# Softplus by one ScalarE function instead of six operations, and the sign of the weights by one VectorE operation, in a retention layer followed by two feed-forward layers

## The chip, the cores and the metric

One core of a Trainium2 chip runs the whole program. The metric is the device time of one launch in microseconds (us), lower is better. The core's engines work side by side, each on its own list of instructions in a fixed order: TensorE (PE) multiplies matrices into PSUM banks, with its weight loads on a row of their own (PEld), VectorE (DVE) and ScalarE (ACT) do the elementwise work, SyncE (SP) issues the DMAs, and GpSimd (POOL) does next to nothing here. An instruction at the head of an engine's list that waits for a semaphore holds up everything behind it on that engine.

## The reference, cut to what matters

```python
# q, k, v: [4, 8, 576, 64]; weights [512, 2048] and [2048, 512], drawn as 64-bit floats
scores = q @ k.transpose(0, 1, 3, 2) / sqrt(64)
ret = (scores * D[None]) @ v               # D[h, i, j] = gamma_h ** (i - j) for i >= j, else 0
x = ret.transpose(0, 2, 1, 3).reshape(2304, 512)
h = x @ moe_w_in
x = (maximum(h, 0) + log1p(exp(-abs(h)))) @ moe_w_out      # softplus
r = maximum(x @ moe2_w_in, 0)
out = (r * r) @ moe2_w_out
```

## The kernel before, in words

The retention runs in chunks of 64 tokens with a carried state. In the first layer every fp32 operand is split into a high part that TensorE's fp32r format holds and a low rest, and a product is three matmuls (high by high, low by high, high by low). Tokens go in five tiles of 512 or 384 (`TILES`). For a tile the work is 16 steps, one for each block of 128 hidden units: `g1` makes a block of h in a PSUM bank named `ph` (12 matmuls), softplus turns it into g, `split_g` into `gh` and `gl`, and `g2` adds it to four output sums named `acc` (12 matmuls). `step` writes this order down by hand: `g1` of step j, softplus of j, a visit to the retention, `split_g` of j - 1, `g2` of j - 2, then weights. The first tile is done in two halves, with the second tile between them, so the order of the tiles is 0 (blocks 0 to 7), 1, 0 (blocks 8 to 15), 2, 3, 4. All but tile 4 is in a manual schedule, where each engine keeps the written order; for tile 4 and what follows, a scheduler picks it.

A visit (`visit`) does one chunk of the retention among the steps: small matmuls `pb` (scores, L388), `po` (outputs, L436) and `st` (state, L413), on VectorE the mask `ring<-pb` (L398), the product `xr<-po` (L459) and the scaling of v (L369, in place in `ring`), and on ScalarE the copy of the state (L424). `pb` takes the PSUM bank that the next `ph` will have, so a bank goes from a block of h to scores and back.

Weights come as 64-bit floats. `words` turns a staged pair of 32-bit words into fp32: ScalarE scales the high word, and multiplies it by a further -2^32 where it is negative (parametric ReLU, L152); ScalarE makes the low bits (L153); VectorE shifts and joins them (L157). `split_w` then makes the high part on ScalarE (L185) and the low part on VectorE (L186). Weights of the second layer go the same way (`split_s`, `split_o`) during tiles 0 to 4. A staging tile (`wi_raw`, `wo_raw`, three buffers) is free for its next load after L157. SP issues these loads and those of `ring` in one queue. In the steps of the first half tile two blocks of weights are made per step, later one or less.

Softplus before is three ScalarE functions in `softplus_a` (Abs L525, Exp L526, Ln L527) and three VectorE operations in `softplus_b` (L532, L535, L538, of which L538 reads `ph` again). Ln writes to tile `l`, a pair of buffers that `drain_one` also uses for stores to DRAM (`xo`).

The last part (`second_phase`) is the second layer, seven products instead of eight by a Strassen scheme. Its code isn't touched.

Of the kernel before, what the change touches and what calls it, by code (L numbers as in the profile page):

```python
# [7 lines left out]
F32 = mybir.dt.float32  # L8
# [3 lines left out]
AF = mybir.ActivationFunctionType  # L12
ALU = mybir.AluOpType
# [3 lines left out]
P = 128  # L17
# [28 lines left out]
def kernel(  # L46
# [26 lines left out]
    nc = tc.nc  # L73
# [19 lines left out]
    ew = ctx.enter_context(tc.tile_pool(name="ew", bufs=2))  # L93
# [14 lines left out]
    below_one = cst[:, C_ONE:C_ONE + 1]  # L108
# [31 lines left out]
    def words(t, ct):  # L140

        y, up, low = t.bitcast(F32)[:, :, 1], t[:, :, 1], t[:, :, 0]
        halves = t.bitcast(U16).rearrange("p a (b two) -> p a b two", two=2)  # L150
        half = halves[:, :, 0, 1]
        nc.scalar.activation(out=y, in_=y, func=AF.Prelu, scale=2.0**-112, alpha=-(2.0**32))  # L152
        nc.scalar.activation(  # L153
            out=low, in_=half, func=AF.Identity, bias=round_up, scale=7.0 / 65535
        )
        yield
        nc.vector.scalar_tensor_tensor(  # L157
            out=ct, in0=up, scalar=3, in1=low,
            op0=ALU.logical_shift_left, op1=ALU.bitwise_or,
        )  # L160
        yield
# [149 lines left out]
    def pump_end():  # L311
        for made in begun:
            while not next(made):
                pass
            pump_load(n_used[0] + STAGES)
        begun.clear()
# [167 lines left out]
    hps = {}  # L484
    tmp = {}
# [27 lines left out]
                ph[:, :n], lhsT=a, rhs=x, start=(j == 0), stop=(j == len(todo) - 1)  # L513
            )

    def softplus_a(key, n):

        ph = hps[key]
        e = ew.tile([P, 512], F32, tag="e", name="e", bufs=3)[:, :n]
        l = ew.tile([P, 512], F32, tag="l", name="l")[:, :n]
        nc.scalar.activation(out=e, in_=ph[:, :n], func=AF.Abs)  # L525
        nc.scalar.activation(out=e, in_=e, func=AF.Exp, scale=-1.0)  # L526
        nc.scalar.activation(out=l, in_=e, func=AF.Ln, bias=below_one, scale=1.0 + 2.0**-23)  # L527
        tmp[key] = (l, e)

    def softplus_b(key, n):  # L530
        l, e = tmp.pop(key)
        nc.vector.scalar_tensor_tensor(  # L532
            out=e, in0=e, scalar=-2.0, in1=e, op0=ALU.add, op1=ALU.mult
        )
        nc.vector.scalar_tensor_tensor(  # L535
            out=l, in0=e, scalar=-0.5, in1=l, op0=ALU.mult, op1=ALU.max
        )
        nc.vector.scalar_tensor_tensor(  # L538
            out=e, in0=hps.pop(key)[:, :n], scalar=0.0, in1=l, op0=ALU.max, op1=ALU.add
        )  # L540
        tmp[key] = e

    def split_g(key, n):
        g = tmp.pop(key)
# [605 lines left out]
    with tc.manual_schedule():  # L1150
# [8 lines left out]
        early_kv(1)  # L1159
        for r in (0, CN):  # L1160
            nc.scalar.dma_start(out=rows_in[r:r + 1], in_=consts[r:r + 1, C_XW:])
        nc.scalar.preload_act_table_set("natural_log_exp_and_others")
        for c in range(2, last):
            early_qk(c)
            early_kv(c)
# [131 lines left out]
    def attend(at_s, i):  # L1297
        rest = None
        while tick[0] < visits(at_s, i):
            if rest:  # L1300
                rest()
            rest = visit(*divmod(tick[0], 2))
            tick[0] += 1
        return rest
# [13 lines left out]
    def step(j, at_s, i):  # L1318
        b, f0, f1 = segments[at_s]
        f = f0 + i  # L1320
        t0, n = TILES[b]
        ends = f == f1 - 1
        if j == 0:
            early_g1(1)
        else:
            g1(j, f, n)
        if at_s == 0 and i < FH - 1:
            pump_end()
        low = []
        if ends and b < last_b:  # L1330
            b1 = segments[at_s + 1][0]
            low = split_x(x_raw.pop(b1), TILES[b1][1])
        softplus_a(j, n)
        later = attend(at_s, i)
        if False and j:
            split_g(j - 1, TILES[steps[j - 1][0]][1])
        for fn in low:
            fn()
        softplus_b(j, n)
        if j and not (False):  # L1340
            split_g(j - 1, TILES[steps[j - 1][0]][1])
        if later:
            later()
        done = g2_parts(j - 2) if j >= 2 else None
        pump_end()
        pump_to(j)
        if j == 0:
            load_chunk(last + 1)
        if done:
            done()  # L1350
        if at_s == 1 and f == KF - 3:
            reload_x()
        if at_s >= 2 and i not in (1, 2):
            n_steps[0] += 1
            goal = -(-18 * NP * n_steps[0] // 46)
            while n_taken[0] < min(18 * NP, goal):
                pump_step()
                n_taken[0] += 1
        if at_s == 3 and i == 0:
            for o in range(KD):  # L1360
                reload_part(o)
        if b == last_b:
            if f == 0:
                second_buffers()
                load_raw(0)
                load_s(4)
            if ends:
                assert n_split[0] == len(items) and not splitting
            for m in range(7):
                if f == GROUP * (m // 2) + GROUP + 1 + m % 2:  # L1370
                    build_t(m)
# [14 lines left out]
    j = len(steps)  # L1386
# [79 lines left out]
```

## Time and profile before

| | |
|---|---|
| three runs | 841.48, 840.74, 837.81 us (median 840.74) |
| profiled execution, first to last instruction (span) | 839.0 us; no time around it is given |
| PE busy | 818.2 us (98%) |
| DVE busy | 702.2 us (84%) |
| ACT busy | 475.3 us (57%) |
| 16 DMA engines, the main queue's share | 71.3% |
| chain of work that ended last | PE 78%, DVE 8%, ACT 8%, DMA 3%, issue 2% |

Busy times are sums over the program, which has stages with different limits; a matmul's end is modelled and overlaps the next one's start, so 98% isn't PE at its peak. PEclk is the granted share of TensorE's clock (0.50 is 1.2 GHz, 1.00 is 2.4 GHz). In a timeline, square brackets hold the time for which the engine was idle before an instruction, and what ended it. Where an instruction waits for several things, the profile names the one that came last by its records.

### The profile page before, as it was taken

To read this page: it belongs to the slowest core of one execution; us is meant where nothing else is said; L and a number is where in the kernel's file an instruction comes from. 1 tells how busy PE (TensorE), PEld (TensorE's weight loads), DVE (VectorE), ACT (ScalarE), POOL (GpSimd) and SP (SyncE) were. 2 spreads that over 40 slices of the span, in tenths; PEclk is the share of its full clock that TensorE was granted. 3 is DMA by queue.
4 is the path that set the end of the run, shared out by engine and by line. 5 is a ranking of instruction groups with operands and counts; after the bars stand their busy time and mean duration, and the time that the engine had idled before them with its cause. 6 is when DMAs were issued, how large, how long until landed. Compare 5 with 4: busy or idle time off the path is not lost.

```text
span 839.0 us, 16498 instructions
## 1 busy us (share of the span) xinstructions
PE 818.2 (98%) x5957; PEld 722.6 (86%) x5957; DVE 702.2 (84%) x1336; ACT 475.3 (57%) x899; POOL 0.2 (0%) x4
## 2 busy tenths in 40 slices
PE   8899999999999998999999999999999999999998
PEld 5677799888788876888799999988999988999887
DVE  4889887878988887787999988999698997787886
ACT  3889888757567667676888521355321554111453
POOL 0000000000000000000000000000000000000000
PEclk9999999999999999999999999999999999999999
DMA  9866544546656665466676688898988889988885
GB/s 234 298 195 235 167 141 145 176 152 214 210 174 198 224 190 176 149 227 202 210 255 219 221 253 249 259 296 275 301 257 245 255 263 280 284 254 252 254 268 176
DMA packets 122804, 189.39 MB, mean 226 GB/s; under 512 B 10466, under 2 KB 68450, under 8 KB 122722
## 3 DMA queue, kind: packets, MB, share of 16 engines
q1 hardware_dynamic: 122560, 188.26, 71.3%
q8 instruction: 47, 0.77, 0.4%
q14 instruction: 33, 0.27, 0.1%
q10 hardware_dynamic: 164, 0.09, 0.1%
HBM read 147.41 MB, written 40.89 MB: 224 GB/s over the span
## 4 chain that ended last, share of the span: by engine, by line
PE 78%; DVE 8%; ACT 8%; DMA 3%; issue 2%; SPq 0%; DVEq 0%; ACTq 0%
PE acc L563 17%; PE ph L512 16%; PE py L699 9%; PE py L772 9%; PE px L699 6%; PE pz L772 6%; PE px L772 6%; PE pz L699 6%; ACT l L527 1%; DMA wi_raw<-in_moe_w_in_dram 1%; DVE l L535 1%; DVE e L532 1%; ACT e L526 1%; ACT e L525 1%; PE po L436 1%
## 5 line engine op out<-in xcount | busy, mean ns | idle before, releaser
L512 PE MATMUL ph<-xh,wi 128*128 128x512 f32 (+1 forms) x632 | 145.1, 371 | 2.2 <-ACT l L527 1.1
L512 PEld LDWEIGHTS ph<-xh,wi 128*128 128x128 f32 x632 | 116.3, 189 | 18.7 <-issue 1.4
L563 PE MATMUL acc<-gl,woh 128*128 128x512 f32 (+1 forms) x320 | 119.0, 372 | 2.9 <-DVE gl L548 2.9
L563 PE MATMUL acc<-gh,woh 128*128 128x512 f32 (+1 forms) x320 | 120.5, 380 | 0.5 <-ACT woh L185 0.5
L563 PE MATMUL acc<-gh,wol 128*128 128x512 f32 (+1 forms) x320 | 118.7, 371 | 0.7 <-DVE wol L186 0.7
L532 DVE SCALAR_TENSOR_TENSOR e<-e 128x512 f32<-128x512 f32 (+1 forms) x80 | 51.0, 638 | 48.7 <-ACT l L527 47.8
L699 PE MATMUL py<-t,sring 128*128 128x384 f32 x432 | 88.6, 339 | 0.0
L525 ACT ACTIVATE e<-ph 128x512 f32<-128x512 f32 (+1 forms) x80 | 44.2, 553 | 60.9 <-PE ph L512 60.4
L512 PE MATMUL ph<-xl,wi 128*128 128x512 f32 (+1 forms) x316 | 77.9, 367 | 0.1
L699 PEld LDWEIGHTS py<-t,sring 128*128 128x128 f32 x432 | 74.8, 188 | 2.6 <-DVE uring L903 0.7
L563 PEld LDWEIGHTS acc<-gl,woh 128*128 128x128 f32 x320 | 60.4, 189 | 12.1 <-DVE gl L548 5.1
L752 ACT CAST gh<-g 128x384 fp32r<-128x384 f32 x84 | 43.1, 515 | 46.6 <-PE px L772 16.7
L563 PEld LDWEIGHTS acc<-gh,woh 128*128 128x128 f32 x320 | 60.4, 189 | 9.8 <-ACT woh L185 0.8
L563 PEld LDWEIGHTS acc<-gh,wol 128*128 128x128 f32 x320 | 60.5, 189 | 8.7 <-DVE wol L186 1.0
L752 ACT CAST gring<-g 128x384 fp32r<-128x384 f32 x84 | 43.1, 514 | 40.3 <-PE py L772 16.4
L512 PEld LDWEIGHTS ph<-xl,wi 128*128 128x128 f32 x316 | 58.1, 188 | 8.0 <-DVE xl L479 0.4
L899 ACT COPY uring<-px 128x384 f32<-128x384 f32 x24 | 11.5, 481 | 87.5 <-PE px L699 87.5
L699 PE MATMUL pz<-t,sring 128*128 128x384 f32 x288 | 58.4, 334 | 0.0
L699 PE MATMUL px<-t,sring 128*128 128x384 f32 x288 | 58.0, 335 | 0.0
L527 ACT ACTIVATE l<-e,cst 128x512 f32<-128x512 f32 (+1 forms) x80 | 54.4, 681 | 5.8 <-DMA x2d<-xo 3.6
L720 DVE TENSOR_TENSOR gring<-g,gring 128x384 fp32r<-128x384 f32 x84 | 46.2, 553 | 10.0 <-ACT gring L752 8.9
L720 DVE TENSOR_TENSOR gl<-g,gh 128x384 fp32r<-128x384 f32 x84 | 46.4, 554 | 9.2 <-ACT gh L752 8.0
(126 smaller groups left out, 1622.3 us busy)
## 6 DMA issues: line engine op xcount, KB each, us to landing
sring<-s2d SPq DMA_DIRECT2D x168, 256.0 KB, 3.2
sring<-o2d SPq DMA_DIRECT2D x168, 256.0 KB, 3.4
wi_raw<-in_moe_w_in_dram SPq DMA_DIRECT2D x32, 512.0 KB, 5.0
wo_raw<-in_moe_w_out_dram SPq DMA_DIRECT2D x32, 512.0 KB, 4.1
s2d<-ct SPq DMA_DIRECT2D x48, 256.0 KB, 2.7
o2d<-ct SPq DMA_DIRECT2D x48, 256.0 KB, 2.6
ring<-in_qk_t_dram SPq DMA_DIRECT2D x14, 512.0 KB, 4.8
ring<-in_kv_dram SPq DMA_DIRECT2D x14, 512.0 KB, 6.1
```

The source lines that it names most:

```text
L436: nc.tensor.matmul(po[(LO, HI)[hh % 2], hh // 2, :], lhsT=before[rows, hh, :] if carried else sv[:, hh, :], rhs=qp[:, hh, :] if carried el ...
L512: nc.tensor.matmul(ph[:, :n], lhsT=a, rhs=x, start=(j == 0), stop=(j == len(todo) - 1))
L525: nc.scalar.activation(out=e, in_=ph[:, :n], func=AF.Abs)
L526: nc.scalar.activation(out=e, in_=e, func=AF.Exp, scale=-1.0)
L527: nc.scalar.activation(out=l, in_=e, func=AF.Ln, bias=below_one, scale=1.0 + 2.0**-23)
L532: nc.vector.scalar_tensor_tensor(out=e, in0=e, scalar=-2.0, in1=e, op0=ALU.add, op1=ALU.mult)
L563: nc.tensor.matmul(acc[j][:, :n], lhsT=a, rhs=x, start=(begin and m == 0), stop=(end and m == 2))
L699: nc.tensor.matmul(ps, lhsT=a, rhs=x, start=(first and m == 0), stop=(m == len(todo) - 1), skip_group_check=True,)
L720: nc.vector.tensor_tensor(out=out, in0=a, in1=b, op=ALU.subtract)
L752: nc.scalar.copy(h, src)
L772: nc.tensor.matmul(blocks[m][:, :cols], lhsT=a[:, c], rhs=x, start=(first and p == n == 0), stop=(p == NP - 1 and n == len(todo) - 1), ski ...
L899: nc.scalar.copy(s1, px)
```

## The change

Softplus becomes one ScalarE function that reads `ph` and writes g. Three VectorE operations and two ScalarE functions per step (80 steps) go. The table of functions that is loaded ahead is another one; ScalarE's parametric ReLU in `words` becomes a scaled copy, and a new VectorE operation, max(-2^32 y, y) in place, stands ahead of the one that joins the words (64 times in all).

```diff
         y, up, low = t.bitcast(F32)[:, :, 1], t[:, :, 1], t[:, :, 0]
...
-        nc.scalar.activation(out=y, in_=y, func=AF.Prelu, scale=2.0**-112, alpha=-(2.0**32))
+        nc.scalar.activation(out=y, in_=y, func=AF.Copy, scale=2.0**-112)
         nc.scalar.activation(
             out=low, in_=half, func=AF.Identity, bias=round_up, scale=7.0 / 65535
         )
         yield
+        nc.vector.scalar_tensor_tensor(
+            out=y, in0=y, scalar=-(2.0**32), in1=y, op0=ALU.mult, op1=ALU.max
+        )
         nc.vector.scalar_tensor_tensor(
             out=ct, in0=up, scalar=3, in1=low,
             op0=ALU.logical_shift_left, op1=ALU.bitwise_or,
...
-    def softplus_a(key, n):
-        ph = hps[key]
-        e = ew.tile([P, 512], F32, tag="e", name="e", bufs=3)[:, :n]
-        l = ew.tile([P, 512], F32, tag="l", name="l")[:, :n]
-        nc.scalar.activation(out=e, in_=ph[:, :n], func=AF.Abs)
-        nc.scalar.activation(out=e, in_=e, func=AF.Exp, scale=-1.0)
-        nc.scalar.activation(out=l, in_=e, func=AF.Ln, bias=below_one, scale=1.0 + 2.0**-23)
-        tmp[key] = (l, e)
-
-    def softplus_b(key, n):
-        l, e = tmp.pop(key)
-        nc.vector.scalar_tensor_tensor(
-            out=e, in0=e, scalar=-2.0, in1=e, op0=ALU.add, op1=ALU.mult
-        )
-        nc.vector.scalar_tensor_tensor(
-            out=l, in0=e, scalar=-0.5, in1=l, op0=ALU.mult, op1=ALU.max
-        )
-        nc.vector.scalar_tensor_tensor(
-            out=e, in0=hps.pop(key)[:, :n], scalar=0.0, in1=l, op0=ALU.max, op1=ALU.add
-        )
-        tmp[key] = e
+    def softplus(key, n):
+        g = ew.tile([P, 512], F32, tag="e", name="e", bufs=3)[:, :n]
+        nc.scalar.activation(out=g, in_=hps.pop(key)[:, :n], func=AF.Softplus)
+        tmp[key] = g
...
-        nc.scalar.preload_act_table_set("natural_log_exp_and_others")
+        nc.scalar.preload_act_table_set("softplus")
...
-        softplus_a(j, n)
+        softplus(j, n)
         later = attend(at_s, i)
...
-        softplus_b(j, n)
         if j and not (False):
             split_g(j - 1, TILES[steps[j - 1][0]][1])
```

In the changed kernel the join is L160 (was L157; its L157 is the new sign operation), high and low part of a weight are L188 and L189 (were L185 and L186), the mask L401 (was L398), `xr<-po` L462 (was L459), the scaling of v L372 (was L369), softplus L526, `split_g` L533 and L534 (were L547 and L548), `g1` L515 and `g2` L549 (were L512 and L563).

Where the order of an engine changes, two places on VectorE matter. The first is the start of the program's steps: low parts of x (`xl<-x,xh`), two blocks of weights, then the masks of the first visits. Before:

```order
L1091 TENSOR_TENSOR xl<-x,xh 128x4x128 x2
L157 SCALAR_TENSOR_TENSOR ct<-wi_raw 128x512 x2
L186 TENSOR_TENSOR wi_392<-ct,wi_392 128x512 x2
L398 TENSOR_TENSOR ring<-pb,cst 64x256 x2
L369 TENSOR_TENSOR ring<-ring,vw 128x512
L398 TENSOR_TENSOR ring<-pb,cst 64x256 x2
L532 SCALAR_TENSOR_TENSOR e<-e 128x512
L535 SCALAR_TENSOR_TENSOR l<-e,l 128x512
L538 SCALAR_TENSOR_TENSOR e<-ph,l 128x512
L157 SCALAR_TENSOR_TENSOR ct<-wo_raw 128x512
```

And in the changed kernel:

```order
L1077 TENSOR_TENSOR xl<-x,xh 128x4x128 x2
L157 SCALAR_TENSOR_TENSOR wi_raw<-wi_raw 128x512
L160 SCALAR_TENSOR_TENSOR ct<-wi_raw 128x512
L157 SCALAR_TENSOR_TENSOR wi_raw<-wi_raw 128x512
L160 SCALAR_TENSOR_TENSOR ct<-wi_raw 128x512
L189 TENSOR_TENSOR wi_393<-ct,wi_393 128x512 x2
L401 TENSOR_TENSOR ring<-pb,cst 64x256 x2
L372 TENSOR_TENSOR ring<-ring,vw 128x512
L401 TENSOR_TENSOR ring<-pb,cst 64x256 x2
L157 SCALAR_TENSOR_TENSOR wo_raw<-wo_raw 128x512
L160 SCALAR_TENSOR_TENSOR ct<-wo_raw 128x512
```

Two sign operations now stand ahead of the first mask (a third stands a little earlier, ahead of the first join), and three softplus operations behind the second pair of masks are gone.

The second place is one step of the first half tile, from a visit's mask to the low parts of the next two blocks of weights. Before:

```order
L398 TENSOR_TENSOR ring<-pb,cst 64x256 x2
L532 SCALAR_TENSOR_TENSOR e<-e 128x512
L535 SCALAR_TENSOR_TENSOR l<-e,l 128x512
L538 SCALAR_TENSOR_TENSOR e<-ph,l 128x512
L548 TENSOR_TENSOR gl<-e,gh 128x512
L459 TENSOR_TENSOR xr<-po,cst 128x256
L369 TENSOR_TENSOR ring<-ring,vw 128x512
L157 SCALAR_TENSOR_TENSOR ct<-wi_raw 128x512
L157 SCALAR_TENSOR_TENSOR ct<-wo_raw 128x512
L186 TENSOR_TENSOR wi_590<-ct,wi_590 128x512
```

And in the changed kernel:

```order
L401 TENSOR_TENSOR ring<-pb,cst 64x256 x2
L534 TENSOR_TENSOR gl<-e,gh 128x512
L462 TENSOR_TENSOR xr<-po,cst 128x256
L372 TENSOR_TENSOR ring<-ring,vw 128x512
L157 SCALAR_TENSOR_TENSOR wi_raw<-wi_raw 128x512
L160 SCALAR_TENSOR_TENSOR ct<-wi_raw 128x512
L157 SCALAR_TENSOR_TENSOR wo_raw<-wo_raw 128x512
L160 SCALAR_TENSOR_TENSOR ct<-wo_raw 128x512
L189 TENSOR_TENSOR wi_584<-ct,wi_584 128x512
```

`gl`, `xr<-po` and the scaling of v come three operations earlier; the weights' operations follow with two more among them. ScalarE's list holds a single ACT_TABLE_LOAD in both kernels.

## Rows read from the trace of the kernel before

**Rows 1.** Busy time by stretch: start:end, length, then PE, PEld, DVE, ACT, POOL, clock.

```profile
24.00:92.00 68.00, 59.25 (x638) 47.37 (x639) 60.80 (x106) 60.70 (x107) 0.00 (x0) 0.95 0.67 226
92.00:410.00 318.00, 312.82 (x2611) 265.09 (x2611) 259.06 (x467) 225.53 (x409) 0.00 (x0) 1.00 0.57 184
410.00:480.00 70.00, 69.77 (x390) 67.47 (x389) 69.03 (x131) 53.72 (x106) 0.00 (x0) 1.00 0.74 237
480.00:839.00 359.00, 355.34 (x2030) 329.54 (x2028) 300.83 (x610) 125.14 (x249) 0.00 (x0) 1.00 0.84 259
```

**Rows 2.** Groups by line: count | busy us, mean ns | idle us before them.

```profile
L525 ACT ACTIVATE e<-ph 128x512 f32<-128x512 f32 (+1 forms) x80 | 44.2, 553 | 60.9 <-PE ph L512 60.4
L526 ACT ACTIVATE e<-e 128x512 f32<-128x512 f32 (+1 forms) x80 | 47.1, 589 | 2.2
L527 ACT ACTIVATE l<-e,cst 128x512 f32<-128x512 f32 (+1 forms) x80 | 54.4, 681 | 5.8 <-DMA x2d<-xo 3.6
L532 DVE SCALAR_TENSOR_TENSOR e<-e 128x512 f32<-128x512 f32 (+1 forms) x80 | 51.0, 638 | 48.7 <-ACT l L527 47.8
L152 ACT ACTIVATE wi_raw<-wi_raw 128x512 f32<-128x512 f32 x32 | 21.5, 671 | 0.5 <-DMA wi_raw<-in_moe_w_in_dram 0.4
L157 DVE SCALAR_TENSOR_TENSOR ct<-wi_raw 128x512 uint32<-128x512 uint32 x32 | 21.7, 685 | 0.7 <-ACT wi_raw L153 0.6
L1162 ACT ACT_TABLE_LOAD x1 | 1.3, 1283 | 3.0 <-issue 3.0
```

**Rows 3.** Timeline of PE, instructions after a pause: start, length, idle before.

```profile
32.38 0.68 PE L388 MATMUL pb<-ring 64*64 64x64 f32 x16 [2.65 <-DVE ring L398]
43.45 0.27 PE L413 MATMUL st<-ring 64*64 64x64 f32 x2 [0.69 <-ACT wo_raw L153]
52.06 0.27 PE L388 MATMUL pb<-ring 64*64 64x64 f32 x2 [0.85 <-DMA ring<-in_qk_t_dram]
73.24 0.27 PE L413 MATMUL st<-ring 64*64 64x64 f32 x2 [1.06 <-ACT wo_raw L153]
164.31 0.27 PE L436 MATMUL po<-ring 64*64 64x64 f32 x2 [0.88 <-DVE xr L459]
213.88 0.27 PE L388 MATMUL pb<-ring 64*64 64x64 f32 x2 [0.82 <-DVE e L538]
317.33 0.94 PE L512 MATMUL ph<-xh,wi 128*128 128x512 f32 x3 [1.03 <-DVE ring L398]
334.14 0.50 PE L563 MATMUL acc<-gl,woh 128*128 128x512 f32 x1 [1.33 <-DVE gl L548]
```

**Rows 4.** Timeline of PE at the change from tile 0 to tile 1.

```profile
85.37 0.51 PE L563 MATMUL acc<-gh,woh 128*128 128x512 f32 x1 [0.47 <-ACT woh L185]
86.75 0.50 PE L563 MATMUL acc<-gl,woh 128*128 128x512 f32 x1 [0.88 <-DVE gl L548]
87.95 0.79 PE L563 MATMUL acc<-gh,wol 128*128 128x512 f32 x1 [0.70 <-DVE wol L186]
...
91.59 0.39 PE L563 MATMUL acc<-gh,wol 128*128 128x512 f32 x1
91.82 0.51 PE L512 MATMUL ph<-xh,wi 128*128 128x384 f32 x2
```

**Rows 5.** Busy time by stretch, 2 us there, the clock's share being 0.50.

```profile
88.00:90.00 2.00, 2.00 (x5) 1.61 (x6) 1.72 (x4) 1.94 (x5) 0.00 (x0) 0.50 0.10 8
```

**Rows 6.** Timeline of DVE ahead of the first masks.

```profile
28.01 0.68 DVE L157 SCALAR_TENSOR_TENSOR ct<-wi_raw 128x512 uint32<-128x512 uint32 x1
29.29 0.69 DVE L157 SCALAR_TENSOR_TENSOR ct<-wi_raw 128x512 uint32<-128x512 uint32 x1 [0.59 <-ACT wi_raw L153]
29.90 1.46 DVE L186 TENSOR_TENSOR wi<-ct,wi 128x512 fp32r<-128x512 f32 x2
31.37 0.86 DVE L398 TENSOR_TENSOR ring<-pb,cst 64x256 f32<-64x256 f32 x2
```

**Rows 7.** Timeline of ACT after the sums of a tile are stored.

```profile
330.59 0.72 ACT L527 ACTIVATE l<-e,cst 128x512 f32<-128x512 f32 x1 [3.47 <-DMA x2d<-xo]
```

## The prediction

> **What bounds the kernel now.** I read the busy time by stretch first. From 480 us on, the second layer, TensorE works without a gap (355 of 359 us) and ScalarE is idle two thirds of the time [rows 1]; nothing that leaves VectorE or ScalarE can shorten it. From 410 to 480 us VectorE is full, 69.03 of 70 us, but so is TensorE, 69.77 of 70 [rows 1]: a full engine beside a full TensorE costs nothing by itself. What is left is 24 to 92 us, where TensorE lacks 8.75 us of 68 and VectorE and ScalarE both work 89% of the time, and 92 to 410 us, where it lacks 5.2 us of 318 [rows 1]. So I looked next for TensorE's pauses, in its timeline, and for what ended each one. The reader is to see in [rows 3, 4] that nearly every pause ends with an operation of VectorE or ScalarE that stood in a queue, and that they are few: the price of this change is read from a dozen places, not from the 254 us of softplus work.
>
> **The change, part by part.**
>
> *Softplus on VectorE.* Three operations per step go, 80 times; one row stands for the three, which have the same form: 80 x 0.638 = 51 us each, 153 us together [rows 2].
>
> *Softplus on ScalarE.* Exp and Ln go, 47.1 + 54.4 = 101.5 us [rows 2]. The new function has no row. It reads the same `ph` and writes the same size as Abs, 553 ns, with constants as Abs has; the dearest function in sight is Ln, 681 ns, which reads a column of `cst` besides [rows 2]. I take 553 (nothing on balance, since Abs goes) and keep 681 (10 us more on ScalarE, off the path) as the upper end; below 553 no row reaches and no row excludes it, but ScalarE's own time is not the term that decides.
>
> *Sign of the weights.* Prelu becomes a scaled copy of the same strided words; its row is 671 ns, and I change nothing (the 589 ns of Exp as a lower end would take 5 us off ScalarE, beside other work). VectorE gets 64 new operations. The nearest row is the join behind it, the same form on the same strided words: 685 ns, 43.8 us in all. The lower end is 638, as the three that go take over both widths, 3 us less in all; an upper end no row gives, and the rival that ends slower takes twice the join. VectorE then falls from 702 to about 593 us, ScalarE from 475 to about 374.
>
> The Trainium skill, "ScalarE: Activation LUTs", section "Rules for kernel authors", advises max and multiply on VectorE, up to about three times faster there in bf16 with one source. In fp32 with two sources the row does not bear it out: 685 ns on VectorE against 671 on ScalarE [rows 2]. By that rule the sign would cost some 0.23 us (an estimate from that page), the head's delay below would be 0.1 us instead of what is taken there, and the time 828.8 us, inside the forecast's own range.
>
> *The head loses.* Ahead of the first mask VectorE now has three sign operations more, and TensorE's second `pb` at 32.38 waits for that mask: 2.65 us idle, ended by L398 [rows 3]. VectorE has one hole there, 0.59 us [rows 6], and is full otherwise. 3 x 0.685 - 0.59 = **1.47 us later**. Ends: 0, if ScalarE and the loads are the slower side, and 2.06, if the hole stays. ScalarE's cast L188 waits for the join, so it is late by the same time, not in addition.
>
> *One step of the first half tile.* VectorE has 3 x 0.638 = 1.91 us less and 2 x 0.685 = 1.37 more: shorter by 0.5 us. ScalarE is shorter by 0.589 + 0.681 = 1.27 us. More to the point is the place: `gl`, `xr` and the scaling of v stand ahead of the sign operations and come 1.9 us earlier. The pauses of 0.69 us at 43.45 and 1.06 at 73.24 are `st` waiting for the scaled v (the profile names L153, long done by then; the operand that comes last in VectorE's order is L369's) [rows 3]. Both are shorter than 1.9 us and go. The pause of 0.85 at 52.06 is a load of `ring` [rows 3]. SP issues it behind a load of weights whose buffer the join frees; the join comes 0.7 us later for the sign and earlier for softplus. I leave that pause as it is; ends -0.85 and +0.8.
>
> *Change from tile 0 to tile 1.* TensorE needs `woh`, `gl` and `wol` in turn and waits for each: 0.47, 0.88 and 0.70 us [rows 4]. After that its clock is granted at 0.50, 1.2 GHz, in all of 88 to 90 us [rows 5]. Twelve matmuls, from 85.37 to 91.82, take 6.45 us; at full clock their starts are 0.23 apart (91.59 to 91.82), 2.76 in all [rows 4]. Lost: 0.47 + 6.45 - 2.76 = **4.16 us**. ScalarE comes there at least two functions' time earlier (two steps, 2.5 us) and VectorE 1.9 us per step less the weights' 1.37; `gl` and `wol` needed to come about 2 us earlier, and both steps' softplus stood ahead of them. So I take the whole 4.16; half of it is the lower end.
>
> *Later tile changes.* 0.88 at 164.31 (VectorE: `xr`, behind three softplus operations), 0.82 at 213.88 (scores wait for L538 to have read `ph`; ScalarE alone reads it now, some 2 us sooner), 1.03 at 317.33 (a mask in VectorE's queue) and 1.33 at 334.14 (`gl`) [rows 3]. The last one has its cause on ScalarE: Ln waited 3.47 us for a store out of tile `l` to land [rows 7], and softplus no longer writes `l`. All four go: each is shorter than the 1.91 us that leave VectorE's queue ahead of it. What is late next is TensorE itself.
>
> *The idle time shown is a little short.* A pause counts from the modelled end of the matmul before, and a matmul of 0.39 us is followed by the next one after 0.23 [rows 4]: 0.16 us more is lost at each. For six pauses (43.45, 73.24 and the four later ones) 0.96 us.
>
> *Hidden edits.* Taking 109 us off VectorE in other places hides under TensorE, whose matmuls follow each other there. In tile 4 the scheduler sets another order, but TensorE is full; if it were worse there by one block of 12 matmuls waiting, it would cost about 1 us.
>
> **Sum:** -(0.69 + 1.06 + 4.16 + 0.88 + 0.82 + 1.03 + 1.33) - 0.96 + 1.47 = -9.46 us. Pauses under half a microsecond at the same lines stand in no row; I round to -10.5 for them. The span goes from 839.0 to 828.5. The median of the runs, 840.74, is 1.74 above that span, and I carry the difference: **830.2 us**.
>
> **The rivals.**
>
> *The tile change at 85 us stays in part.* The weights' words still come late there: two sign operations and two joins stand ahead of `wol`, and the clock drops after any long pause as it did [rows 5]. Against it: the weights were not the last of the three. Without the 4.16 us: 840.74 - 6.3 = 834.4.
>
> *New waits eat the rest.* The pauses go where VectorE set them, but the loads (52.06) come later by 0.8 at each of the four `ring` loads of the first half tile, 3.2 us, and the tile change keeps half: -10.5 + 3.2 + 2.1 = -5.2; with the head at its end of 2.06 and 213.88 and 317.33 kept, 838.
>
> *Slower: the sign operation makes the first half tile VectorE's.* It stands between ScalarE's low bits and the casts L188, so ScalarE idles for it, twice per step, and the masks stand behind. The point from which it decides: two sign operations cost as much as three softplus ones when each takes 0.96 us instead of 0.685. If reading and writing the same strided words in place took twice the join, 1.37 us: 2 x 1.37 - 1.91 = 0.83 us more per step, 6.6 in eight steps; the head loses 3 x 1.37 - 0.59 = 3.5, and its pause of 2.65 + 3.5 would hold the clock down longer, as after 87.95, where that cost 6.45 - 2.76 - 0.88 - 0.70 - 2 x 0.16 = 1.8 us. The tile change stays, the four later pauses go (-4.06 - 0.64). Sum +7.2: 847.9. For it: both engines are 89% busy there. Against it: the join with the same form and stride takes 685.
>
> *The change isn't what it says: tables are swapped.* One table is loaded, 1.28 us, in the whole program [rows 2]. If softplus and its neighbours sat in different tables, two loads per step for 80 steps would be 160 x 1.28 = 205 us on ScalarE; of this 2.57 us per step would meet a full engine in the first half tile, +20 us or more, 860. ScalarE's order in the changed kernel holds one load, which speaks against it.
> The Trainium skill, "ScalarE: Activation LUTs", section "Table sets: the hidden batching unit", tells to group calls by set, since each switch costs a load and a drain; by its 2.7 us per switch the estimate would be twice that. No row here shows a switch.
>
> **How the numbers follow.** 0.5% of 840.74 is 4.2 us, about what a measurement can tell from no change: faster means under 836.5, slower over 844.9. Forecast (826 to 833): 0.65. Tile change stays (832 to 836): 0.2. New waits (836 to 841): 0.09. Slower: 0.05. Tables: 0.01. The ends of the head, the `ring` load and the unseen pauses reach down to 825. The range is 824.5 to 836.5; over it are left about 0.13, under it about 0.05. Faster 0.86, same 0.1, slower 0.04.
>
> **What would show it.** In the changed profile: 80 functions at L526 of about 553 ns; 64 sign operations of about 685; ACT near 374 and DVE near 593 us; the second `pb` at about 33.9 us instead of 32.38; no pause over 0.3 us at the change to tile 1 and a clock of 1.00 there; no wait of ScalarE for a store of `xo` at the end of a tile; TensorE's starts in the second layer as before, only earlier. I am wrong if the pauses of [rows 3, 4] are there with other names behind them, or if the sign operation takes far more than 685 ns.

## The result and the profile after

| | before | after |
|---|---|---|
| median of the runs | 840.75 us (837.81 to 841.48) | 825.77 us (4 runs, 825.59 to 827.56) |
| profiled execution, own time; span | -; 839.0 us | 825.89; 824.1 us |
| PE, DVE, ACT busy | 818.2, 702.2, 475.3 us | 811.5, 607.8, 378.8 us |

The ratio of after to before is 0.983, 95% interval 0.9814 to 0.9846. The runs moved by 15.0 us and the two spans by 14.9, where 10.5 had been forecast. 825.77 lies inside the range of 824.5 to 836.5, at its low end.

The profile's page of the changed kernel begins as follows (busy time, share of the span, instructions), and its chain that ended last is TensorE's for 96% of the span, where it was 78%.

```profile
PE 811.5 (98%) x5957; PEld 723.0 (88%) x5957; DVE 607.8 (74%) x1160; ACT 378.8 (46%) x739; POOL 0.2 (0%) x4
```

Busy time by stretch, in the columns and over the stretches of [rows 1]; the last stretch ends with the span:

```profile
24.00:92.00 68.00, 62.77 (x666) 51.91 (x667) 60.34 (x105) 52.67 (x96) 0.00 (x0) 0.95 0.73 237
92.00:410.00 318.00, 318.00 (x2653) 272.59 (x2652) 194.50 (x357) 161.69 (x310) 0.00 (x0) 1.00 0.61 195
410.00:480.00 70.00, 70.00 (x405) 69.82 (x404) 50.28 (x88) 32.81 (x63) 0.00 (x0) 1.00 0.70 221
480.00:824.00 344.00, 340.25 (x1945) 315.59 (x1943) 290.05 (x589) 121.22 (x241) 0.00 (x0) 1.00 0.83 260
```

From 92 to 480 us TensorE has no idle time left, where it lacked 5.2 and 0.2 us. In 24 to 92 us it still lacks 5.2 of the 8.75 us. VectorE is as full there as before, 60.34 of 68 us, because the sign operations came in and the same time now holds more of the program's steps.

The groups by line that answer to [rows 2]:

```profile
L526 ACT ACTIVATE e<-ph 128x512 f32<-128x512 f32 (+1 forms) x80 | 44.3, 553 | 127.2 <-PE ph L515 127.0
...
L160 DVE SCALAR_TENSOR_TENSOR ct<-wi_raw 128x512 uint32<-128x512 uint32 x32 | 22.2, 693 | 2.9
...
L157 DVE SCALAR_TENSOR_TENSOR wo_raw<-wo_raw 128x512 f32<-128x512 f32 x32 | 22.0, 688 | 2.8 <-ACT wo_raw L152 2.8
L157 DVE SCALAR_TENSOR_TENSOR wi_raw<-wi_raw 128x512 f32<-128x512 f32 x32 | 22.0, 687 | 0.0
L152 ACT ACTIVATE wi_raw<-wi_raw 128x512 f32<-128x512 f32 x32 | 21.7, 678 | 0.7 <-DMA wi_raw<-in_moe_w_in_dram 0.6
```

Softplus as one function takes 553 ns, exactly what Abs took. The sign operation takes 687 ns against 685 forecast. The scaled copy takes 678 where Prelu took 671: nothing is won on ScalarE there. ScalarE's wait for a store, 3.6 us at L527 in [rows 2], is gone; softplus now waits for TensorE, 127.0 of its 127.2 us.

Of the pauses of [rows 3, 4] one is left. The second shown here has no row there, though the kernel before had it, too. TensorE's timeline:

```profile
33.73 1.12 PE L391 MATMUL pb<-ring 64*64 64x64 f32 x16 [3.49 <-DVE ring L401]
34.78 3.78 PE L515 MATMUL ph<-xh,wi 128*128 128x512 f32 x8
...
41.79 1.39 PE L515 MATMUL ph<-xh,wi 128*128 128x512 f32 x5 [1.07 <-DVE ring L401]
```

The first is the pause of 2.65 us, longer and later. The second, 1.07 us, stood at 39.76 in the kernel before and was as long there; Ln ended it then, a mask ends it now. Why the head came later is read from VectorE's timeline, to be laid beside [rows 6]:

```profile
28.52 0.69 DVE L157 SCALAR_TENSOR_TENSOR wi_raw<-wi_raw 128x512 f32<-128x512 f32 x1
29.25 0.69 DVE L160 SCALAR_TENSOR_TENSOR ct<-wi_raw 128x512 uint32<-128x512 uint32 x1
29.86 0.69 DVE L157 SCALAR_TENSOR_TENSOR wi_raw<-wi_raw 128x512 f32<-128x512 f32 x1
30.65 0.69 DVE L160 SCALAR_TENSOR_TENSOR ct<-wi_raw 128x512 uint32<-128x512 uint32 x1
31.26 1.46 DVE L189 TENSOR_TENSOR wi<-ct,wi 128x512 fp32r<-128x512 f32 x2
32.73 0.86 DVE L401 TENSOR_TENSOR ring<-pb,cst 64x256 f32<-64x256 f32 x2
```

The hole of 0.59 us is filled, and the mask starts at 32.73 instead of 31.37: 1.36 us later. The clock shows what is lost there besides. Stretches of 2 us, clock in the third column from the end:

```profile
32.00:34.00 2.00, 0.27 (x5) 0.30 (x7) 1.92 (x4) 1.41 (x3) 0.00 (x0) 0.50 1.17 316
36.00:38.00 2.00, 2.00 (x6) 1.52 (x6) 1.21 (x3) 0.62 (x1) 0.00 (x0) 0.50 0.97 393
38.00:40.00 2.00, 2.00 (x34) 1.42 (x36) 0.65 (x1) 0.34 (x1) 0.00 (x0) 0.81 0.86 287
88.00:90.00 2.00, 2.00 (x11) 1.70 (x10) 1.18 (x3) 1.46 (x4) 0.00 (x0) 1.00 0.89 231
```

The granted clock is 0.50, 1.2 GHz, from 32 to 38 us, and the block of 12 matmuls from 34.78 takes 4.78 us, where one at full clock takes 2.8 to 3.0. In the kernel before, the clock was at 0.50 in all of 34 to 36 us only, and the same block, from 32.99, took 4.53. The stretch from 88 to 90 us, 0.50 in [rows 5], is at full clock, and so is all of 40 to 92 us, in which the change to tile 1 now stands at 83 to 86.

**Where the time went.** The start of each block of matmuls in the one trace set against its start in the other gives the shift along the program:

| place (time before) | forecast, us | measured, us |
|---|---|---|
| head, up to 39.76 | +1.47 | +2.03 |
| pauses at 43.45 and 52.06 | -0.85, the second unchanged | -1.96 |
| pause at 73.24 | -1.22 | -1.39 |
| change to tile 1, 77 to 92 | -4.16 | -4.33 |
| 164.31 | -1.04 | -0.96 |
| 209 to 217 | -0.98 | -1.49 |
| 309 to 317 | -1.19 | -1.96 |
| 330 to 342 | -1.49 | -1.63 |
| all the rest, to the end | -1.04 | -3.48 |
| sum | -10.5 | -15.2 |

(A forecast pause has its 0.16 us for the modelled end added. The sum is taken from matmul to matmul, 0.3 us more than from span to span.) The shift is -14.8 by 473 us and hardly moves in the second layer, as forecast.

### The profile page after: what moved, and what is told of

It reads as the page before. It is cut to its first block, busy times and chain, and to the rows that moved or that the text cites. A ratio compares the mean times of both kernels' runs of the same rounds, so it can differ in the third digit from the quotient of the medians.

```text
span 824.1 us, 16242 instructions
## 1 busy us (share of the span) xinstructions
PE 811.5 (98%) x5957; PEld 723.0 (88%) x5957; DVE 607.8 (74%) x1160; ACT 378.8 (46%) x739; POOL 0.2 (0%) x4
## 4 chain that ended last, share of the span: by engine, by line
PE 96%; DMA 2%; DVE 1%; ACT 0%; issue 0%; SPq 0%; DVEq 0%
PE acc L549 25%; PE ph L515 24%; PE py L685 9%; PE py L758 9%; PE px L685 6%; PE pz L758 6%; PE px L758 6%; PE pz L685 6%; PE po L439 2%; DMA qk<-in_qk_t_dram 1%; PE pb L391 1%; PE st L416 1%; DMA kv<-in_kv_dram 1%; SPq L970 0%; DVE wi_raw L157 0%
## 5 line engine op out<-in xcount | busy, mean ns | idle before, releaser
L515 PE MATMUL ph<-xh,wi 128*128 128x512 f32 (+1 forms) x632 | 144.5, 371 | 1.1 <-DVE ring L401 1.1
L515 PEld LDWEIGHTS ph<-xh,wi 128*128 128x128 f32 x632 | 116.5, 190 | 16.5 <-PE pb L391 1.2
L549 PE MATMUL acc<-gh,woh 128*128 128x512 f32 (+1 forms) x320 | 120.6, 377 | 0.0
L549 PE MATMUL acc<-gh,wol 128*128 128x512 f32 (+1 forms) x320 | 117.9, 368 | 0.0
L549 PE MATMUL acc<-gl,woh 128*128 128x512 f32 (+1 forms) x320 | 117.9, 368 | 0.0
L534 DVE TENSOR_TENSOR gl<-e,gh 128x512 fp32r<-128x512 f32 (+1 forms) x80 | 51.0, 637 | 71.2 <-ACT gh L533 70.4
L526 ACT ACTIVATE e<-ph 128x512 f32<-128x512 f32 (+1 forms) x80 | 44.3, 553 | 127.2 <-PE ph L515 127.0
L515 PE MATMUL ph<-xl,wi 128*128 128x512 f32 (+1 forms) x316 | 77.8, 368 | 0.0
L549 PEld LDWEIGHTS acc<-gh,woh 128*128 128x128 f32 x320 | 60.1, 188 | 8.5
L549 PEld LDWEIGHTS acc<-gh,wol 128*128 128x128 f32 x320 | 60.1, 188 | 7.7
L549 PEld LDWEIGHTS acc<-gl,woh 128*128 128x128 f32 x320 | 60.2, 188 | 6.8
L515 PEld LDWEIGHTS ph<-xl,wi 128*128 128x128 f32 x316 | 58.2, 189 | 7.5
L401 DVE TENSOR_TENSOR ring<-pb,cst 64x256 f32<-64x256 f32 x56 | 23.6, 421 | 44.3 <-PE pb L391 29.3
L706 DVE TENSOR_TENSOR g<-g 128x384 f32<-128x384 f32 x96 | 52.6, 555 | 1.5
```

The costliest lines, as they stand in the source:

```text
L401: nc.vector.tensor_tensor(out=chunk[c][rows, 1, i * HH:(i + 1) * HH], in0=pb[of], in1=mask[of], op=ALU.mult)
L515: nc.tensor.matmul(ph[:, :n], lhsT=a, rhs=x, start=(j == 0), stop=(j == len(todo) - 1))
L526: nc.scalar.activation(out=g, in_=hps.pop(key)[:, :n], func=AF.Softplus)
L534: nc.vector.tensor_tensor(out=l[:, :n], in0=g, in1=h[:, :n], op=ALU.subtract)
L549: nc.tensor.matmul(acc[j][:, :n], lhsT=a, rhs=x, start=(begin and m == 0), stop=(end and m == 2))
L706: nc.vector.tensor_tensor(out=out, in0=a, in1=b, op=ALU.subtract)
```

## The experiments

Two theories had to be told apart. **The queue theory**, on which the prediction rests: what counts is how many VectorE operations stand ahead of `gl`, `xr`, the scaled v, the masks and the casts' joins, so nearly all of the gain comes from softplus leaving VectorE. **Its rival**: ScalarE's two functions per step count as much, since both engines are 89% busy in the first half tile.

**1. The changed kernel without the sign operation.** It leaves the sign out, so negative weights get a wrong scale.

```diff
-        nc.vector.scalar_tensor_tensor(
-            out=y, in0=y, scalar=-(2.0**32), in1=y, op0=ALU.mult, op1=ALU.max
-        )
```

> The changed kernel without the 64 sign operations (negative weights keep a wrong scale; what else runs is the same). If the sign costs time only ahead of the first mask: the mask starts about 1.4 us earlier (31.3 instead of 32.73), less of the first block runs at half clock, and the time is 1.4 to 2.3 us below 825.8: 823.5 to 824.4. If the sign is hidden even there (loads or ScalarE set the head): 825.5 to 826. If it also costs time in each step of the first half tile: below 822.

Measured: 823.45 us (822.67 to 826.84), ratio to before 0.9803, interval 0.9781 to 0.9825. The pause in the head is 2.65 us again, at 32.06. The blocks run 2.1 us ahead of the changed kernel's at its 34.78 and 2.4 to 2.8 from there to the end. So the 64 sign operations, 44 us of VectorE, cost 2.3 us by the medians, nearly all of it in the first 35 us: the three ahead of the first mask pay, and what the other 61 cost is a few tenths. The interval overlaps that of the changed kernel (0.9814 to 0.9846), so that the place of the cost, and a part of its size, rest on one trace of each.

**2. The kernel before with the sign operation alone.**

```diff
-        nc.scalar.activation(out=y, in_=y, func=AF.Prelu, scale=2.0**-112, alpha=-(2.0**32))
+        nc.scalar.activation(out=y, in_=y, func=AF.Copy, scale=2.0**-112)
...
+        nc.vector.scalar_tensor_tensor(
+            out=y, in0=y, scalar=-(2.0**32), in1=y, op0=ALU.mult, op1=ALU.max
+        )
```

> The kernel before with the sign moved to VectorE, softplus as it was. If VectorE's queue sets TensorE's pauses, as the prediction has it: VectorE's step in the first half tile grows by 1.37 us on an engine that is 89% busy there, the head is late by 1.4 to 2 us, the later pauses grow by 0.7 us where words stand in the step: 848 to 856 us. If the sign is hidden beside ScalarE's work: 841 to 843.

Measured: 861.79 us (858.53 to 863.29), ratio 1.0239, interval 1.0212 to 1.0266: 21 us slower than before, above the expected range. TensorE's timeline and two stretches of it:

```profile
51.70 0.47 PE L515 MATMUL ph<-xh,wi 128*128 128x512 f32 x1 [0.88 <-DVE ring L401]
...
98.75 0.69 PE L566 MATMUL acc<-gl,woh 128*128 128x512 f32 x1 [1.98 <-DVE gl L551]
```

```profile
24.00:92.00 68.00, 53.93 (x613) 41.31 (x609) 60.36 (x102) 50.45 (x89) 0.00 (x0) 0.95 0.61 197
92.00:410.00 318.00, 306.25 (x2554) 255.82 (x2554) 279.54 (x496) 221.69 (x402) 0.00 (x0) 0.99 0.54 174
```

The masks are now late at four steps (four waits of `ph` for L401, 3.7 us, in 24 to 92 us), the wait for `gl` at the tile change grows from 0.88 to 1.98, and TensorE lacks 14.1 us in the first stretch and 11.8 in the second. The same 64 operations cost 21 us where VectorE's queue still holds three operations of softplus per step, and ScalarE's two more functions, and 2.3 where both are gone.

**3. The changed kernel with three VectorE operations put back**, at the place where softplus had them, chosen so that the result stays the same.

```diff
+        for _ in range(2):
+            nc.vector.scalar_tensor_tensor(
+                out=e, in0=e, scalar=1.0, in1=e, op0=ALU.mult, op1=ALU.max
+            )
+        nc.vector.scalar_tensor_tensor(
+            out=e, in0=hps.pop(key)[:, :n], scalar=0.0, in1=e, op0=ALU.max, op1=ALU.max
+        )
```

> The changed kernel with three VectorE operations of softplus's old form and place put back (they leave g as it is; the last one reads ph again), ScalarE as in the change, tile l not used. Theory of VectorE's queue: nearly all of the gain goes, and with the sign on top the first half tile is worse than before: 840 to 850 us, pauses at the change to tile 1 and at the later ends of tiles are back, only the one that waited for a store out of tile l stays away. Rival, that ScalarE's two functions were what TensorE waited for: 827 to 833.

Measured: 848.43 us (846.06 to 848.93), ratio 1.0087, interval 1.007 to 1.0103: 22.7 us above the changed kernel, as the queue theory had it. Most of the pauses of [rows 3, 4] are back with the same releasers, in TensorE's timeline:

```profile
95.23 0.50 PE L559 MATMUL acc<-gl,woh 128*128 128x512 f32 x1 [1.98 <-DVE gl L544]
96.44 0.50 PE L559 MATMUL acc<-gh,wol 128*128 128x512 f32 x1 [0.70 <-DVE wol L189]
...
173.50 0.27 PE L439 MATMUL po<-ring 64*64 64x64 f32 x2 [1.10 <-DVE xr L462]
```

Those for `woh` (85.37) and for the reading of `ph` (213.88) don't come back, and late masks and state copies hold `ph` up six times, 5.3 us in 24 to 92 us. At 95 us of the changed kernel the shift against it is 14.8 us. The long one of 334.14 with its wait for a store does not come back, since tile `l` isn't there.

**4. The changed kernel with two ScalarE functions put back.**

```diff
+        for _ in range(2):
+            nc.scalar.activation(out=g, in_=g, func=AF.Relu)
```

> The changed kernel with two ScalarE functions (max with 0, which leaves g as it is) put back behind softplus, VectorE as in the change. Theory of VectorE's queue: 826 to 828.5, the pauses stay away except part of the one at the change to tile 1, where ScalarE's cast was one of the three that TensorE waited for. Rival, that ScalarE's time was what counted: 833 to 838.

Measured: 835.23 us (833.98 to 836.13), ratio 0.9934, interval 0.9919 to 0.9949: 9.5 us above the changed kernel. Here the rival is right. Of the 9.5, 7.0 have come by 93 us (about 1 of it from the start of the profiled run, before the change acts), the rest in the tiles behind 399 us. TensorE waits again for a load of `ring` and for `woh`, in its timeline:

```profile
55.53 0.27 PE L391 MATMUL pb<-ring 64*64 64x64 f32 x2 [1.31 <-DMA ring<-in_qk_t_dram]
...
89.24 0.50 PE L551 MATMUL acc<-gh,woh 128*128 128x512 f32 x1 [0.42 <-ACT woh L188]
```

Neither theory is enough by itself. The runs make a table (medians; rows and columns say what of the softplus work remains, or its like in number and nearly in duration; the sign operation is on VectorE in all four):

| | 3 on VectorE | none on VectorE |
|---|---|---|
| 2 more on ScalarE | 861.8 (run 2) | 835.2 (run 4) |
| none more | 848.4 (run 3) | 825.8 (the change) |

Leaving VectorE is worth 26.6 or 22.7 us, leaving ScalarE 13.4 or 9.4, both 36.0; less the sign's 21.0 that is the change's 15.0. VectorE's part is the larger by two to one. (Run 2 alone still has the store out of tile `l`, which run 7 below prices at 1.3 us, so its row and column hold that too.)

**5. Prelu kept with the new softplus**, so that the tables must be swapped.

```diff
-        nc.scalar.activation(out=y, in_=y, func=AF.Copy, scale=2.0**-112)
+        nc.scalar.activation(out=y, in_=y, func=AF.Prelu, scale=2.0**-112, alpha=-(2.0**32))
...
-        nc.vector.scalar_tensor_tensor(
-            out=y, in0=y, scalar=-(2.0**32), in1=y, op0=ALU.mult, op1=ALU.max
-        )
```

> The changed kernel with the sign left to ScalarE's parametric ReLU (no VectorE operation for it). Prelu isn't in softplus's table, so ScalarE swaps tables: its list holds 103 table loads instead of 1, two per step of the first tiles. With the row's 1.283 us each, 131 us more on ScalarE: in the first half tile 2.57 us per step on an engine that does 53 of 68 us in the change, so about 73 of 68 are wanted there: 8 to 14 us, and little later, where ScalarE does 162 of 318: 833 to 842 us. If a swap costs twice its row (by the Trainium skill's ScalarE page about 2.7 us with the drain): 850 us and more. If swaps are hidden everywhere: 824 to 826.

Measured: 851.73 us (850.17 to 852.23), ratio 1.0133, interval 1.0114 to 1.0152. ScalarE's timeline around one pair of swaps, then the groups of loads:

```profile
63.25 0.62 ACT L185 CAST woh<-ct 128x512 fp32r<-128x512 f32 x1 [0.25 <-DVE ct L157]
63.89 1.28 ACT L523 ACT_TABLE_LOAD   x1
65.19 0.60 ACT L523 ACTIVATE e<-ph 128x512 f32<-128x512 f32 x1
...
67.09 1.28 ACT L152 ACT_TABLE_LOAD   x1
68.39 0.69 ACT L152 ACTIVATE wi_raw<-wi_raw 128x512 f32<-128x512 f32 x1
```

```profile
L152 ACT ACT_TABLE_LOAD x51 | 65.4, 1283 | 4.6 <-DMA wo_raw<-in_moe_w_out_dram 3.7
L523 ACT ACT_TABLE_LOAD x51 | 65.4, 1283 | 6.3 <-PE ph L512 5.5
```

There are 102 swaps of 1.283 us, with, in this pair, the operation ahead ending 0.02 us before the load and the next beginning 0.02 after it. The time is above the range that I had worked out from this duration all the same: 16.1 us are lost by 100 us of the changed kernel and 9.3 more by 160, at waits such as these in TensorE's timeline, for ScalarE's cast and for a mask:

```profile
99.09 0.50 PE L546 MATMUL acc<-gh,woh 128*128 128x512 f32 x1 [1.62 <-ACT woh L185]
...
137.26 0.94 PE L512 MATMUL ph<-xh,wi 128*128 128x384 f32 x4 [1.83 <-DVE ring L398]
```

The Trainium skill, "ScalarE: Activation LUTs", section "What ACT_TABLE_LOAD costs", puts a switch at a load and a drain, some 2.7 us together; the trace agrees with its load and shows no time for a drain. That the sum came near the estimate by 2.7 us is therefore no support for it. What follows: the sign operation is the price of keeping ScalarE in one table, and a cheap one; with Prelu and its swaps in its place the kernel is 26 us slower.

**6. The head's order changed**: the first mask ahead of wi1's low part, wi2's words behind the second mask.

```diff
-        for made in begun:
-            next(made)
+        next(begun[0])
         early_keep(3)
...
             tick[0] += 1
+            if at_s == i == 0 and len(begun) == 2:
+                made = begun.pop(0)
+                while not next(made):
+                    pass
...
-        if at_s == 0 and i < FH - 1:
+        if at_s == 0 and 0 < i < FH - 1:
```

> The changed kernel with another order at the start: the first visit's mask stands ahead of the low part of the first of the two weight blocks, and the second block's words stand behind the second mask. Theory of VectorE's queue at the head: the mask starts at 30.2 to 30.5 us instead of 32.73, TensorE's pause of 3.49 falls to about 1, less of the first block runs at half clock: 2.5 to 5 us less, 820.8 to 823.3. Rival, that loads set the head (the queue's transfers take 0.8 to 1.2 of the DMA engines there): 825 to 826, with TensorE waiting for ring or for weights instead.

Measured: 829.05 us (827.05 to 830.82), ratio 0.9859, interval 0.9831 to 0.9887: a miss, 3.3 us above the changed kernel. TensorE's timeline, then that of SP's DMA queue:

```profile
33.77 0.68 PE L391 MATMUL pb<-ring 64*64 64x64 f32 x16 [1.05 <-DVE ring L401]
42.19 0.27 PE L391 MATMUL pb<-ring 64*64 64x64 f32 x2 [4.07 <-DMA ring<-in_qk_t_dram]
43.92 1.19 PE L515 MATMUL ph<-xh,wi 128*128 128x512 f32 x2 [1.05 <-DVE ring L401]
```

```profile
37.23 0.33 SPq L137 DMA_DIRECT2D wo_raw<-in_moe_w_out_dram  x1
37.60 0.42 SPq L362 DMA_DIRECT2D ring<-in_qk_t_dram  x1
```

The head's pause did fall, from 3.49 to 1.05 us. But wi2's words now free their staging buffer late (their join stands at 36.47 on VectorE, 29.25 or 30.65 in the changed kernel), a load of weights waits for that buffer on SP, and the load of `ring` stands behind it (37.60, where the changed kernel issues it at 31.75). Not all of the miss is the order's: in this execution the loads of the first chunks landed late, and TensorE is 2.4 us behind the changed kernel by 14.8 us, while no engine's order differs before 29.9. Of the 4.7 us by which the blocks are late at 52 us that leaves 2.3; without it the first mask, 32.76, would stand at the 30.2 to 30.5 expected. I had moved VectorE's work without asking which transfer its end releases.

**7. The kernel before, with the odd stores of a tile's sums out of another tile than softplus's `l`.**

```diff
-            o = ew.tile([P, 512], F32, tag="l", name="xo")[:, :n]
+            o = cvt.tile([P, 512], F32, tag="ct", name="xo")[:, :n]
```

> The kernel before, with the stores at the end of a tile taken out of another pool than Ln's tile l. If that store alone caused the pause of 1.33 at 334: ScalarE's wait of 3.47 us for x2d<-xo and TensorE's pause are gone, 1.5 us less: 838.5 to 839.8. If VectorE's queue caused it: the pause stays, 840 to 841.5.

Measured: 839.5 us (10 runs, 836.57 to 841.26), ratio 0.9975, interval 0.9956 to 0.9993. ScalarE's group of Ln, beside [rows 2]:

```profile
L527 ACT ACTIVATE l<-e,cst 128x512 f32<-128x512 f32 (+1 forms) x80 | 54.5, 681 | 2.3
```

Its idle time falls from 5.8 to 2.3 us with no store among its causes, the pause of 334.14 is gone, and the blocks behind it run 1.5 us earlier: the store was the cause, and the prediction's 1.49 its price.

**8. The head's order of run 6, with the next load of `ring` issued in the head; 9, that load alone.**

```diff
         early_keep(3)
+        load_chunk(last + 1)
...
-        if j == 0:
-            load_chunk(last + 1)
```

> The head order of the sixth run, with the loads of the visit after next (ring<-in_qk_t_dram, ring<-in_kv_dram) issued in the head, ahead of the first step, so that they stand ahead of the weight load that waits for a staging buffer. Queue theory (the pause of 4.07 us at 42.19 in the sixth run was only that place on SP): the pause goes, and with it the half clock of the block behind it, so that 4.7 us and up to 2.5 us of clock are won against the sixth run's 829.05, and the sign's 2.4 us of head come back without touching a computation: 820.8 to 823.5, under the changed kernel. Rival (the ring's data is late for another reason: staging buffers or the DMA engines are full): a pause of over 1.5 us stays between 40 and 48 us and the time is 825 to 829.

> Control: the changed kernel with only the early ring loads, the head's order as it was. Its trace has no pause by the ring's DMA left (that of 52.06 in the kernel before is gone by itself), so the queue theory expects nothing: 825 to 827. If the loads, issued 8 us earlier, get in the way of the weights or of the x loads, 827.5 to 830, with a new DMA pause between 35 and 50 us.

Measured: run 8 takes 825.83 us (825.08 to 828.53; ratio 0.9843, interval 0.9825 to 0.9861), run 9 826.88 us (825.37 to 828.01; ratio 0.9843, interval 0.9828 to 0.9858). The control stays within the 825 to 827 expected of it. In run 8 the wait for the DMA is gone, and 3.2 us are won against run 6 (in the traces 4.2 by 52 us, of which 1.7 are the earlier start). But a pause of nearly the same length stands 1.3 us earlier, and the time is the 825 to 829 of the rival, though it isn't the load of `ring` that is late. TensorE's timeline and VectorE's:

```profile
32.02 0.68 PE L391 MATMUL pb<-ring 64*64 64x64 f32 x16 [1.05 <-DVE ring L401]
40.90 1.36 PE L515 MATMUL ph<-xh,wi 128*128 128x512 f32 x3 [4.16 <-ACT ring L427]
```

```profile
37.01 0.69 DVE L157 SCALAR_TENSOR_TENSOR wo_raw<-wo_raw 128x512 f32<-128x512 f32 x1 [0.22 <-ACT wo_raw L152]
37.81 0.69 DVE L160 SCALAR_TENSOR_TENSOR ct<-wo_raw 128x512 uint32<-128x512 uint32 x1
39.19 0.69 DVE L189 TENSOR_TENSOR wol<-ct,woh 128x512 fp32r<-128x512 f32 x1 [0.68 <-ACT woh L188]
39.89 0.86 DVE L401 TENSOR_TENSOR ring<-pb,cst 64x256 f32<-64x256 f32 x2
```

The third mask, whose scores ended at 36.7, waits behind the split of a wo pair. (The profile names the copy of the state, L427, as what ended TensorE's pause; it ended at 40.80, the mask at 40.75.) That pair comes later because the two loads of `ring` now stand ahead of its own load on SP: it is issued at 29.76 and ScalarE begins on it at 36.31, in the changed kernel at 27.86 and 33.18.

**10. Run 8, with each wo pair begun one step later in the first three steps.**

```diff
-        pump_begin(4 + 2*j if j<FH else 3+2*FH+(j-FH))
+        pump_begin((3 if j < 3 else 4) + 2*j if j<FH else 3+2*FH+(j-FH))
```

> The eighth run, with each split of a wo pair begun one step later in the first three steps (the wo's words stood ahead of the third mask, whose work of 0.86 us began at 39.89 though its scores had ended at 36.5). Queue theory: the third mask starts at about 37, the pause of 4.16 us at 40.90 falls to 1.0 to 1.5 and the half clock behind it goes; a part comes back as a later pause, since the wo's split must still be done for the first products of the second layer (up to 1.5 us). 821.5 to 824. Rival (VectorE is simply full between 30 and 50 us, 15.43 us busy of 18 in the eighth run, so that every order pays the two added sign operations and only the place of the pause moves): 825 to 827.5, with pauses of 4 us or more in all between 30 and 60 us.

Measured: 824.57 us (822.85 to 826.34), ratio 0.9817, interval 0.9791 to 0.9843. TensorE's timeline:

```profile
31.45 0.68 PE L391 MATMUL pb<-ring 64*64 64x64 f32 x16 [1.05 <-DVE ring L401]
38.84 2.08 PE L515 MATMUL ph<-xh,wi 128*128 128x512 f32 x8 [1.07 <-DVE ring L401]
...
50.58 0.27 PE L391 MATMUL pb<-ring 64*64 64x64 f32 x2 [0.76 <-DMA ring<-in_qk_t_dram]
```

The pauses did what the queue theory said: 4.16 fell to 1.07, and at 48.7 us of the changed kernel the program runs 2.44 us ahead of it. But 2.2 of those are given back by 66 us, to two waits of 0.76 and 0.69 us for loads of `ring` and to short ones. The time lies between the two ranges expected, and TensorE idles for 3.1 us between 30 and 60 us, less than the rival's 4. The median is 1.2 us under the changed kernel's, and the two intervals overlap: faster than before, yes; faster than the change, not shown.

## Why the prediction was right, and where it was off

**Right: what bounds, and where.** Each pause listed in [rows 3, 4] went, but for the head's, and the stretches from 480 us on only moved. Reading a dozen pauses instead of the 254 us of softplus work gave the time to 4.4 us, of a change of 15.0: the way and the places were right, and the size two thirds of what came.

**Right: durations.** 553 ns and 687 to 688 ns were forecast from the rows of Abs and of the join to 3 ns. The sums by line fell as forecast, VectorE's by 106 us and ScalarE's by 99. Their busy time fell less, to 607.8 and 378.8 instead of 593 and 374: instructions that follow each other overlap (`L189` at 33.65 and `L372` at 34.26 in run 6 are 0.61 us apart and 0.69 long), and the busy time counts the overlap once. A sum of durations is too much by that for an engine that works without a gap. The slower rival's sign operation of twice the join isn't there. Its mechanism, a first half tile that is VectorE's, is real, though, and run 2 shows its price when nothing is taken off: 12.6 us by the change to tile 1, 21 in all.

**Right in size, not in all its parts: the head.** 1.36 us at the mask against 1.47. By 39.76 us it had become 2.03, since the clock stays at 0.50 for a longer time; the step left out the clock, which the slower rival had in its sum. That the longer pause is the cause isn't shown: in run 7, the kernel before but for a store, the clock is at 0.50 in all of 32 to 38 us behind a pause of 2.64.

**Right: the change to tile 1.** -4.33 us against 4.16, with the clock at 1.00 as said. The reason given, that ScalarE comes earlier too, is supported by run 4: with ScalarE's two functions back, `woh` is waited for again, 0.42 us at 89.24.

**Mis-sized: "Pauses under half a microsecond at the same lines stand in no row; I round to -10.5 for them."** This term of 1.04 us measured 3.48 (the table's last row but one), and at 209 to 217 and 309 to 317 the change gave 0.5 and 0.8 us more than the listed pauses there. The stretches of [rows 1] held more of it: TensorE lacked 5.2 us from 92 to 410, of which the listed pauses are 4.06. They did not hold all: from 92 to 403 us of the kernel before, the shift grows by 7.8. A gap behind a modelled end shows shorter than it is. Everything that waited for VectorE or ScalarE was going to go, small waits as well.

**Mis-sized: "I leave that pause as it is"**, of the load at 52.06. It went (the two pauses of 43.45 and 52.06 gave 1.96 us, 0.85 forecast). The forecast had the end of -0.85 in its range. It was weighed by when the load is issued, 46.56 us now and 46.21 before; but TensorE came to it 1.1 us later in the new program, and so did not wait. The same pause has 1.06 us in run 9 and 0.43 in run 7, so it depends on where TensorE stands by a few tenths.

**Mis-sized: "ScalarE's own time is not the term that decides."** The 1.27 us per step that leave ScalarE stood in the sum only at the tile change; run 4 prices them at 9.5 us, most of it by 93 us.

What stays open: which of the short waits at 311, 399 and 411 to 420 us are VectorE's and which ScalarE's, as no run takes them one by one.

## What to carry to other kernels

An operation has no price of its own: 64 sign operations cost 21 us in a full queue and 2.3 where three operations per step had gone from it, and two functions from ScalarE's, so a trade between engines must be costed with both halves in place. When all waits of one kind will go, take the lack of busy time of the bound engine over the stretch as the least that can come, and not the sum of the pauses that are long enough to be listed (from 92 to 410 us 5.2 against 4.06, and 7.8 came). Before work is put later on an engine, list the buffers that it frees and the transfers that stand behind them in the queue; runs 6, 8 and 10 took a pause of 3.5 us away three times and met it again at the next place twice.

## What was not expected of the hardware

A table load costs 1.283 us and next to nothing around it, over the 102 swaps of run 5, as far as ScalarE's idle times tell (10.9 us of idle time ahead of all of them, 9.2 of it ended by a DMA or by TensorE).

After the pause of 3.49 us the granted clock was 0.50 for 6 us and more, and so it was in run 7 after 2.64; after 2.65 in the kernel before it was 0.50 in 34 to 36 us and 0.86 in the next two; after 1.05 us at the same place in run 8 it was 1.00 up to 40 us, and then 0.50 from 42 to 44 behind the pause of 4.16. In run 10 it fell to 0.50 in 34 to 36 us though TensorE had idled for only 1.05 there, at 31.45; what is different from run 8 in that stretch I could not find. The stretch in run 8, then the one in run 10:

```profile
34.00:36.00 2.00, 2.00 (x35) 1.44 (x37) 1.39 (x2) 0.55 (x1) 0.00 (x0) 1.00 1.03 384
```

```profile
34.00:36.00 2.00, 2.00 (x6) 1.57 (x5) 1.28 (x3) 0.62 (x1) 0.00 (x0) 0.50 0.92 324
```
